# Order at the head of attention, ScalarE in emission order, and routing steps that carry over, in a fused attention and expert kernel

## The chip, the cores and the metric

One core of one Trainium2 chip. The metric is the device time of one execution in microseconds (us), median over the runs of one kernel. Every batch of experiments ran beside fresh runs of the kernel before, on the same chip.

## The reference, cut to what matters

Sliding-window attention (8 batches, 8 heads, 576 positions, head size 64, window 64) is followed by a layer of 8 experts. Each of the 4608 rows goes to exactly one expert, which depends on the row's logits and, by a second "local" gate, on the expert of the row before it.

```python
attn_out = _attn_ref(q, k, v)                      # softmax over 64 earlier positions
x = attn_out.transpose(0, 2, 1, 3).reshape(B, S, H * D)
logits = x @ w_gate;  local_gate = sigmoid(x @ w_local)
for b in range(B):
    prev_e = -1
    for s in range(S):
        fresh_e = argmax(logits[b, s])
        e = fresh_e if s == 0 or local_gate[b, s] < 0.5 else prev_e
        prev_e = e
        h = relu(x[b, s] @ w1[e])
        out[b, s] = softmax(logits[b, s])[e] * (h @ w2[e])
```

## The kernel before

Attention runs over 9 superchunks of 512 rows, each in 4 units (pairs of heads). A unit's scores are emitted two units ahead of its values. The gate logits come from `vt`, a second, turned copy of v that only the gates read. The values also read `vb`, v moved by 64 positions, which ScalarE copies. After half of the rows are done, the routing of the first half (which row goes to which expert, as a table `idx`) is worked off in 15 pieces, squeezed between the attention units. Then the rows of the first expert block are gathered by an indirect DMA with `idx`, and the experts run.

```python
HALF = 0.8
...
def turned(sc):                                   # vt of a superchunk, one buffer
    vtt = vts[sc] = kp.tile([P, HP, SC], F32, name="vtt", bufs=1)
    nc.sync.dma_start(out=vtt, in_=vt[:, :, sc * SC:(sc + 1) * SC])
turned(0); load(0); load(1)                       # load: k and q by pairs, then v3
...
gated = gates(0)                                  # TensorE, reads vt; copy on ScalarE
turned(1)
for move in spread(0, *gated): move()             # transposes, then the vb copies on ScalarE
units = [(sc, hp) for sc in range(NSC) for hp in range(HP)]
ps = {u: scores(*u) for u in units[:LEAD]}        # the first scores and exponentials

def step():                                       # called twice in each unit
    nonlocal pause
    if side and pause <= 0:
        pause = next(side, (0.0, False))[0]       # a routing piece, with its weight in us
    pause -= HALF

for i, (sc, hp) in enumerate(units):
    ...                                           # scores of unit i + 2, vb copies
    step(); values(sc, hp, ...)
    if hp == 0: gated = gates(sc + 1); turned(sc + 2)
    step()
    if hp == HP - 1:
        ...                                       # store of the superchunk's rows to xs, on GpSimd's queue
        if side is None and 4 * (sc + 1) >= C1: side = rt.first(psum)
for _ in side:                                    # what is left of the routing
    pass
ex.begin()                                        # gathers and weights of the first two expert blocks
```

The four tiles of the buffer ring hold k and q of the superchunks first and expert weights afterwards. So the second block's weights (two matrices of 2 MB) can only be loaded when the last scores are done, at about 142 us. At the end a flag is tested, and a slow fallback path follows in a branch that isn't taken.

## Time and profile before

| | |
|---|---|
| time, median of 3 runs | 752.04 us (751.59 to 752.31) |
| span in the profile | 750.2 us |
| TensorE busy | 691.8 us, 92% |
| routing table ready, gather issued | 147.97, 148.25 us |
| last attention matmul ends | 148.67 us |
| first expert matmul | 161.26 us |
| last matmul of the program | 742.42 us |

Read the table as two stages with a hole between them. TensorE is full in the expert stage, so only an earlier start of it can shorten the run. The start hangs on a chain: the table, the gather, the transposes of the gathered rows. The lines that show this are in the prediction.

### The profile page before, as it was taken

To read this page: it belongs to the slowest core of one execution; us is meant where nothing else is said; L and a number is where in the kernel's file an instruction comes from. 1 tells how busy PE (TensorE), PEld (TensorE's weight loads), DVE (VectorE), ACT (ScalarE), POOL (GpSimd) and SP (SyncE) were. 2 spreads that over 40 slices of the span, in tenths; PEclk is the share of its full clock that TensorE was granted. 3 is DMA by queue.
4 is the path that set the end of the run, shared out by engine and by line. 5 is a ranking of instruction groups with operands and counts; after the bars stand their busy time and mean duration, and the time that the engine had idled before them with its cause. 6 is when DMAs were issued, how large, how long until landed. Compare 5 with 4: busy or idle time off the path is not lost. (4 is left out here: it accounts for less than half of the span.)

```text
span 750.2 us, 12553 instructions
## 1 busy us (share of the span) xinstructions
PE 691.8 (92%) x5479; PEld 502.4 (67%) x5479; DVE 182.7 (24%) x426; ACT 145.8 (19%) x186; POOL 92.8 (12%) x109
## 2 busy tenths in 40 slices
PE   3788787749999999999999999999999999999995
PEld 2666666647677767567567567576776777677673
DVE  4576788923730011011010010010010001001000
ACT  2667665401111101101101101100110110010010
POOL 2000000111132111111110110111111111010010
PEclk9799999969999999999999999999999999999998
DMA  9999996867889964644654643689889898888601
GB/s 327 388 393 399 395 388 251 321 245 251 325 313 382 423 268 142 241 178 140 231 186 139 225 187 141 216 308 348 307 332 328 307 343 307 319 295 310 225 15 31
DMA packets 37331, 203.84 MB, mean 272 GB/s; under 512 B 3437, under 2 KB 3453, under 8 KB 29072
## 3 DMA queue, kind: packets, MB, share of 16 engines
q1 hardware_dynamic: 28320, 173.45, 63.1%
q0 software_dynamic: 8944, 29.45, 9.9%
q8 instruction: 47, 0.77, 0.4%
q14 instruction: 20, 0.16, 0.1%
HBM read 184.01 MB, written 19.92 MB: 272 GB/s over the span
## 5 line engine op out<-in xcount | busy, mean ns | idle before, releaser
L872 PEld LDWEIGHTS hp<-xt,w 128*128 128x128 f32 x2048 | 274.8, 193 | 28.3 <-issue 14.3
L872 PE MATMUL hp<-xt,w 128*128 128x128 f32 (+1 forms) x2048 | 289.9, 303 | 0.7 <-ACT xt L860 0.7
L886 PE MATMUL yp<-w,h 128*128 128x512 f32 x640 | 280.4, 592 | 0.0
L886 PEld LDWEIGHTS yp<-w,h 128*128 128x128 f32 x640 | 118.9, 190 | 136.8 <-issue 134.9
L876 DVE TENSOR_SCALAR h<-hp 128x512 f32<-128x512 f32 x34 | 23.5, 691 | 473.5 <-issue 362.0
L891 ACT ACTIVATE y<-yp,pw 128x512 f32<-128x512 f32 x40 | 27.5, 687 | 358.3 <-PE yp L886 342.2
L892 POOL DMA_INDIRECT out_dram<-y,idx x40 | 41.8, 1045 | 302.6 <-ACT y L891 275.8
L840 POOL DMA_INDIRECT xg<-xs,idx x40 | 39.1, 977 | 217.3 <-PE tp L859 188.4
L878 ACT ACTIVATE h<-hp 128x512 f32<-128x512 f32 x46 | 27.5, 597 | 163.0 <-PE hp L872 163.0
L238 PE MATMUL sp<-w 64*64 64x128 f32 (+1 forms) x1296 | 46.4, 278 | 13.7 <-issue 8.4
L238 PEld LDWEIGHTS sp<-w 64*64 64x64 f32 x1296 | 39.7, 142 | 22.8 <-issue 14.4
L267 PE MATMUL xo<-vb,p 128*64 128x74 f32 x576 | 46.8, 233 | 8.3 <-issue 4.3
L267 PEld LDWEIGHTS xo<-vb,p 128*64 128x64 f32 x576 | 40.8, 138 | 11.5 <-issue 4.8
L267 PE MATMUL xo<-va,p 128*64 128x74 f32 x576 | 47.0, 234 | 1.5 <-issue 1.5
L257 DVE TENSOR_TENSOR p<-p,mask 128x1024 f32<-128x1024 f32 x36 | 43.9, 1221 | 12.1 <-ACT p L254 11.9
L267 PEld LDWEIGHTS xo<-va,p 128*64 128x64 f32 x576 | 40.8, 138 | 2.7 <-issue 2.7
L254 ACT ACTIVATE p<-sp 128x1024 f32<-128x1024 f32 x36 | 36.7, 1022 | 15.7 <-PE sp L238 14.1
L859 PE MATMUL tp<-ident,xg 128*128 128x128 f32 x160 | 23.2, 277 | 10.8 <-DMA xg<-xs,idx 10.8
L859 PEld LDWEIGHTS tp<-ident,xg 128*128 128x128 f32 x160 | 18.9, 143 | 11.8 <-issue 11.0
L209 PE MATMUL xo<-vtt,wg2s 128*32 128x512 f32 x72 | 12.5, 705 | 13.9 <-DMA wg2s<-in_wg_dram 8.3
L276 DVE TENSOR_TENSOR x<-xo,allr 128x512 f32<-128x512 f32 x36 | 24.5, 680 | 0.0
L322 POOL DMA_DIRECT2D xs<-x x9 | 6.9, 764 | 130.3 <-DVE x L276 116.2
(198 smaller groups left out, 201.5 us busy)
## 6 DMA issues: line engine op xcount, KB each, us to landing
w<-in_w_dram SPq DMA_DIRECT2D x64, 2048.0 KB, 8.7
va<-in_v_dram SPq DMA_DIRECT2D x9, 1184.0 KB, 12.6
vtt<-in_vt_dram SPq DMA_DIRECT2D x9, 1024.0 KB, 11.1
xs<-x POOLq DMA_DIRECT2D x9, 1024.0 KB, 10.2
w<-in_k_dram SPq DMA_DIRECT2D x8, 1024.0 KB, 13.1
w<-in_q_dram SPq DMA_DIRECT2D x8, 1024.0 KB, 15.0
w<-in_k_dram SPq DMA_DIRECT2D x4, 256.0 KB, 6.1
w<-in_q_dram SPq DMA_DIRECT2D x4, 256.0 KB, 5.8
```

What stands on the lines that cost most here:

```text
L238: nc.tensor.matmul(sp[c * WIN:(c + 1) * WIN, j, a:b], lhsT=kt[h, hp, block * WIN:(block + 1) * WIN], rhs=qt[h, hp, a:b], start=True, stop= ...
L254: nc.scalar.activation(p, sp, Act.Exp, scale=DH ** -0.5)
L257: nc.vector.tensor_tensor(p, p, m.to_broadcast([P, 2, SC]), op=Alu.mult)
L267: nc.tensor.matmul(xo[par * WIN:(par + 1) * WIN, j, s * VW:(s + 1) * VW], lhsT=p[:, j, b * WIN:(b + 1) * WIN], rhs=w[:, s, 2 * hp + j, :], ...
L276: nc.vector.tensor_tensor(x[:, :, hp].rearrange("p c j d -> p j c d"), o[:, :, :, :DH], rr.to_broadcast([P, 2, 4, DH]), op=Alu.mult)
L840: nc.gpsimd.indirect_dma_start(out=x, out_offset=None, in_=self.xs[:rows, :], in_offset=bass.IndirectOffsetOnAxis(ap=idx[:, s:s + 1], axis=0))
L859: nc.tensor.transpose(tp[:, kk, :], x[:, kk * P:(kk + 1) * P], self.ident)
L872: nc.tensor.matmul(hp[:, i, :], lhsT=st["w1"][:, kk, m * P:(m + 1) * P], rhs=st["xt"][:, kk, :n], start=(kk == 0), stop=(kk == DK - 1))
L878: nc.scalar.activation(o, hp, Act.Relu)
L886: nc.tensor.matmul(yp, lhsT=st["h"][:, m, i * P:(i + 1) * P], rhs=st["w2"][:, m, :], start=(m == 0), stop=(m == FK - 1))
L891: nc.scalar.activation(y, yp, Act.Copy, scale=st["pw"][:, s:s + 1])
L892: nc.gpsimd.indirect_dma_start(out=self.out[:, :], out_offset=bass.IndirectOffsetOnAxis(ap=st["idx"][:, s:s + 1], axis=0), in_=y, in_offse ...
```

## The change

It has four parts. The routing steps carry their remaining allowance over to the next call (before, a `pause` below zero was overwritten and so lost), and the first fetch moves into the loop. The first two units' scores are emitted before the first gates, and the small gate weights are loaded earlier. ScalarE keeps the order in which the program emits its instructions. The loads of a superchunk are ordered by need.

```diff
+    wg2s = const.tile([P, HP, GW], F32, name="wg2s")     # moved up from behind zrow
+    nc.gpsimd.dma_start(out=wg2s, in_=wg2)
...
-    ctx.enter_context(tc.manual_schedule(engines={ET.PE}))
+    ctx.enter_context(tc.manual_schedule(engines={ET.PE, ET.Activation}))
...
-    turned(0)
-    load(0)
-    load(1)
+    load(0, [slice(0, 1), slice(1, 2), "turned", "values", slice(2, 3), slice(3, 4)])
+    load(1, ["values", pairs])
...
+    units = [(sc, hp) for sc in range(NSC) for hp in range(HP)]
+    ps = {u: scores(*u) for u in units[:LEAD]}
     gated = gates(0)
-    turned(1)
+    load(1, ["turned"])
     for move in spread(0, *gated):
         move()
-    units = [(sc, hp) for sc in range(NSC) for hp in range(HP)]
-    ps = {u: scores(*u) for u in units[:LEAD]}
...
     def step():
-        nonlocal pause
-        if side and pause <= 0:
-            pause = next(side, (0.0, False))[0]
+        nonlocal pause, side
         pause -= HALF
+        if side and pause <= 0.0:
+            w, trip = next(side, (0.0, None))
+            pause = max(pause, -HALF) + w
+            if trip is None:
+                side = ()
+                ex.begin()
...
-            if sc + 2 < NSC:
-                load(sc + 2)                              # at the head of the superchunk
...
             if sc + 2 < NSC:
-                turned(sc + 2)
+                load(sc + 2, ["turned", "values", pairs])
...
-    for _ in side:
-        pass
-    ex.begin()
+    while side:
+        step()
```

More of the change, by code (lines that the diff above doesn't have):

```diff
@@ L94 @@
     ok = const.tile([P, 1], F32, name="ok")
-    wg2s = const.tile([P, HP, GW], F32, name="wg2s")
-    nc.gpsimd.dma_start(out=wg2s, in_=wg2)
     moe = xs, w1, w2, out, tabs, lt, ident
@@ L154, in attention, with load @@
     ps_x = ctx.enter_context(tc.tile_pool(name="at_ps_x", bufs=2, space=PSUM))
-    ctx.enter_context(tc.manual_schedule(engines={ET.PE}))
+    ctx.enter_context(tc.manual_schedule(engines={ET.PE, ET.Activation}))
     qts, kts, vts, vas, vbs = {}, {}, {}, {}, {}
-    def load(sc):
+    def load(sc, parts):
         t = slice(sc * SC, (sc + 1) * SC)
-        both = ring.tile([P, 2, HP, SC], F32, name="w")
-        kt, qt = kts[sc], qts[sc] = both[:, 0], both[:, 1]
-        va = vas[sc] = kp.tile([P, 4, H, VW], F32, name="va")
-        step = 1 if sc == 0 else HP
-        for i in range(0, HP, step):
-            h = slice(i, i + step)
-            nc.sync.dma_start(out=kt[:, h], in_=k[:, h, t])
-            nc.sync.dma_start(out=qt[:, h], in_=q[:, h, t])
-        nc.sync.dma_start(out=va, in_=v3[t].rearrange("(c p) h x -> p c h x", p=P))
-    def turned(sc):
-        vtt = vts[sc] = kp.tile([P, HP, SC], F32, name="vtt", bufs=1)
-        nc.sync.dma_start(out=vtt, in_=vt[:, :, sc * SC:(sc + 1) * SC])
-    turned(0)
-    load(0)
-    load(1)
+        for part in parts:
+            if part == "turned":
+                vtt = vts[sc] = kp.tile([P, HP, SC], F32, name="vtt", bufs=1)
+                nc.sync.dma_start(out=vtt, in_=vt[:, :, t])
+            elif part == "values":
+                va = vas[sc] = kp.tile([P, 4, H, VW], F32, name="va")
+                nc.sync.dma_start(out=va, in_=v3[t].rearrange("(c p) h x -> p c h x", p=P))
+            else:
+                if sc not in kts:
+                    both = ring.tile([P, 2, HP, SC], F32, name="w")
+                    kts[sc], qts[sc] = both[:, 0], both[:, 1]
+                nc.sync.dma_start(out=kts[sc][:, part], in_=k[:, part, t])
+                nc.sync.dma_start(out=qts[sc][:, part], in_=q[:, part, t])
+    pairs = slice(0, HP)
+    load(0, [slice(0, 1), slice(1, 2), "turned", "values", slice(2, 3), slice(3, 4)])
+    load(1, ["values", pairs])
     row = cp.tile([P, 1], I32, name="row")
```

## The prediction

> **What bounds the kernel now.** I read the page's slices first, then busy time by engine in stretches, then the instructions in order of time around the place where attention hands over to the experts.
>
> ```profile
> PE   3788787749999999999999999999999999999995
> PEclk9799999969999999999999999999999999999998
> DMA  9999996867889964644654643689889898888601
> ```
>
> One digit is 18.8 us. From slice 9 (about 169 us) to the end TensorE never falls below 90%: this is the expert stage, and its length is TensorE's work. No part of the change touches it, so it can only start earlier. All that can be won lies in the first eight or nine slices. Stretches of that part (columns: length, PE, PE weight load, DVE, ACT, POOL busy, clock, DMA share, GB/s):
>
> ```profile
> 20.00:100.00 80.00, 64.61 (x1536) 52.09 (x1536) 55.04 (x107) 52.38 (x57) 3.80 (x5) 0.94 1.04 394
> 100.00:120.00 20.00, 15.53 (x367) 12.48 (x367) 16.78 (x47) 13.09 (x14) 0.75 (x1) 1.00 1.01 378
> 126.00:140.00 14.00, 10.02 (x244) 8.07 (x247) 13.54 (x35) 7.77 (x8) 0.75 (x1) 1.00 0.98 370
> 150.00:160.00 10.00, 0.50 (x3) 0.53 (x4) 2.50 (x10) 0.00 (x0) 1.41 (x2) 0.61 1.01 414
> 160.00:165.00 5.00, 4.32 (x20) 3.92 (x19) 0.90 (x5) 0.91 (x2) 0.97 (x1) 0.50 0.28 93
> ```
>
> Until 100 us the DMA engines are full (1.04, 394 GB/s) and ScalarE is busy only 52.4 of 80 us; from 126 to 140 us VectorE is the full one (13.54 of 14); from 150 to 160 us nothing computes. That hole is the largest single loss:
>
> ```profile
> 141.78 0.75 POOL L322 DMA_DIRECT2D xs<-x  x1 [13.60 <-DVE x L276]
> 148.25 1.04 POOL L840 DMA_INDIRECT xg<-xs,idx  x1 [5.72 <-DVE idx L730]
> 159.50 1.08 PE L859 MATMUL tp<-ident,xg 128*128 128x128 f32 x4 [10.83 <-DMA xg<-xs,idx]
> 161.26 6.06 PE L872 MATMUL hp<-xt,w 128*128 128x128 f32 x32 [0.68 <-ACT xt L860]
> 167.37 3.74 PE L872 MATMUL hp<-xt,w 128*128 128x128 f32 x32
> ```
>
> The last attention matmul ends at 148.67. TensorE then waits 10.83 us for the gathered rows of the first expert block. The gather was issued at 148.25, when the routing table (idx) was ready, and landed 11.1 us later. The first block's weights were in time: issued at 125.2 and 128.7, landed after 9.5 and 12.5 us, so by 141.2. The first 32 expert matmuls take 6.06 us, the next equal 32 take 3.74.
>
> At the head:
>
> ```profile
> 8.26 1.94 PE L209 MATMUL xo<-vtt,wg2s 128*32 128x512 f32 x8 [8.26 <-DMA wg2s<-in_wg_dram]
> 12.01 3.70 PE L238 MATMUL sp<-w 64*64 64x128 f32 x72
> 20.00 1.94 ACT L254 ACTIVATE p<-sp 128x1024 f32<-128x1024 f32 x2
> 26.38 1.93 PE L209 MATMUL xo<-vtt,wg2s 128*32 128x512 f32 x8 [1.14 <-DMA vtt<-in_vt_dram]
> ```
>
> Gates, scores and the vb copies stand in a row before the first exponential at 20.0. At 26.38 TensorE waits for the second superchunk's vt.
>
> **What the Trainium skill says.** "TensorE: Matmul & The Clock Gate", Part 1, gives half the clock after an idle window of about 3.4 us and the full clock again after as long a busy one. The trace agrees: 0.50 in 160 to 165 us, and 6.06 against 3.74 us. "DMA: Bandwidth & Descriptors", Issuing engines are not separate DMA queues, says that all issuers share the same 16 DMA engines. The trace agrees: the gather shared them with 4 MB of weights issued at 142 and a 1 MB store. The same page, Two DMAs through the same engine are not ordered, says that descriptors of one queue start in order; here the store issued at 141.78 landed after 16.4 us (158.2), and the gather behind it on the same queue at 159.3. "Runtime: NRT & Kernel Launch", Instruction fetch mechanics, says instructions are refilled in 16 KiB blocks and this is mostly hidden. The page shows 47 such packets; TensorE has unexplained gaps of 0.8 to 1.8 us about every 6.4 us while the DMA engines are full, which would fit refills that are not hidden. No run shows that cause, and the change doesn't touch it.
>
> **The change part by part.** Instruction counts, matmuls and bytes stay the same; I take no time off for work removed.
>
> 1. Routing steps that carry over. Each step of the routing has a weight in us, each call pays 0.8. Before, a remainder below zero was thrown away. Counted from the code with the 15 weights (sum 17.8): the last piece comes out at call 30 of 32 before, at call 23 after. Two calls make a unit, calls start in unit 20. So idx moves from just after unit 34 to just before unit 31's normalisation; the built program's VectorE order says the same. Fetching the first blocks also moves inside the loop, and on GpSimd's queue the two gathers now stand ahead of the store of superchunk 7, not behind it. The stretch from idx to the last attention matmul: before, unit 31's normalisation at 140.81 to 148.67, or 7.9 us, of which 0.9 was the table's end; estimate 7 to 7.5. A gather that isn't behind a store landed in 3.1 us (issued at 160.9) to 7.9 us (beside weights). It should land just before or at the end of attention. Then TensorE runs on: transposes 0.7, copy 0.6, hand-overs 0.15, so the first expert matmul starts 1.45 us after 148.67, at 150.1 in place of 161.26: 11.1 us. With no gap of over 3 us the clock stays up: 6.06 - 3.74 = 2.3 us. Sum 13.4 us.
>
> 2. Scores before gates, vt no longer first, wg2s first. The head's chain gets shorter: scores can start at about 6 us, exponentials are no longer behind the vb copies, and I estimate the first values at 17 in place of 23.0. But the gates of superchunk 1 stand next in TensorE's order and need vt of superchunk 1. Ahead of it in the queue are the same 7.7 MB as before (two superchunks of k, q, v3 and one vt). At 0.39 MB per us it lands at 26.4 before and within 0.5 us of that after. So 6 us are won and waited away. I count 0.3.
>
> 3. ScalarE in emission order. Before, three vb copies (1.18 each) often ran ahead of an exponential. Until 97 us TensorE never waited for it: its gaps there are of the unexplained kind. After 97 us VectorE waited for exponentials 0.74 + 0.32 + 0.34 + 0.43 = 1.8 us; I take half, 0.9.
>
> 4. Loads in the order of need. From superchunk 5 the built queue again reads k, q, v3, vt, as before; earlier vt moves ahead of q. With a full queue and 48 MB in all no byte comes sooner on the whole. 0.
>
> 5. VectorE from unit 20 to 35. Its work (about 50 us out of 55) is unchanged, only squeezed to the front; it stays the bound from 100 to 148 us. Denser PSUM round trips of the routing may cost as much as calmer last units give. 0, give or take 2.
>
> Sum: 13.4 + 0.3 + 0.9 = 14.6. I hold back 0.3 for a gather that sometimes lands late: 14.3. Predicted time 752.04 - 14.3 = 737.7 us, 1.9% less.
>
> **The rivals.** (a) The head's 6 us survive to the end of attention: 732. For it: DVE and ACT get earlier work. Against: DMA at 1.04 until 112 us, and the wait for vt at 26.38. (b) The gather lands late still, as its packets meet the second block's weights, issued after the last scores (142.1 before): 3 to 6 us of the hole stay, 741 to 744. Against: those weights need about 10 us, and the gather is ahead of them. (c) The squeezed routing makes TensorE and VectorE wait for each other through the two shared PSUM buffers: attention ends 2 to 3 us later, 740. For it: five round trips in calls 3 to 8 in place of 5 to 11. (d) Emission order blocks exponentials behind a copy that waits; a us or two.
>
> **Range and chances.** The 13.4 us are a measured hole and sure to 1.5 us; the attention stretch is open by 2 to 3 us either way. 80%: 733.5 to 741.5. The border of 2% is at about 737.1, just below my number: faster 0.45, within 2% 0.54, slower 0.01.
>
> **What would show it.** Right: no wait of TensorE for xg over 1.5 us; the first 32 expert matmuls in about 3.7 us; idx about 7 us before the last attention matmul; the expert stage about 579 us from its first matmul, the start of which is near 149; the first values at 17 but the second gates still at about 26, waiting for vt. Wrong: second gates well before 25 us (a); an xg wait of several us (b); the last attention matmul after 150 (c, d), or before 146.

## The result

The changed kernel takes 739.10 us (median of 4 runs, 737.77 to 740.69); the runs of the kernel before beside it have a median of 751.82. The ratio is 0.9834, with a 95% interval of 0.9811 to 0.9858. A ratio is the mean time of one kernel's fast runs over the mean of the other's in the same rounds, so it isn't quite the ratio of the medians quoted. The result is correct, and by the border of 2% the verdict is "within 2%".

The slices of the page after (40 slices of 18.4 us, digits in tenths):

```profile
PE   5588878899999999999999999999999999999995
PEclk9999999999999999999999999999999999999999
DMA  9999999699899965455355446588998898888500
```

The dip to 4 at slice 8 of before is gone: TensorE is at 90% or more from slice 8 on. The place of the hand-over, from the timelines of GpSimd and TensorE (start, duration, engine, line and operation, idle time before it and what ended it):

```profile
141.84 1.04 POOL L841 DMA_INDIRECT xg<-xs,idx  x1 [11.61 <-DVE allr L272]
145.22 0.82 POOL L324 DMA_DIRECT2D xs<-x  x1
...
146.66 0.65 PE L860 MATMUL tp<-ident,xg 128*128 128x128 f32 x4
150.13 3.81 PE L873 MATMUL hp<-xt,w 128*128 128x128 f32 x32 [1.21 <-ACT xt L861]
154.00 3.74 PE L873 MATMUL hp<-xt,w 128*128 128x128 f32 x32
```

The second block's weights in SyncE's queue, first before, then after:

```profile
142.12 1.02 SPq L846 DMA_DIRECT2D w<-in_w_dram  x2
```

```profile
143.57 1.02 SPq L847 DMA_DIRECT2D w<-in_w_dram  x2
```

The gather goes out 6.4 us earlier (141.84 against 148.25), and now 1.7 us ahead of these weights, not 6.1 us behind them. It lands after 3.6 us in place of 11.1. Its rows are there when TensorE reaches the transposes (no wait on that line), and the transposes even fit in ahead of the last attention matmuls, which end at 148.93. What is left of the hole is 1.21 us for the copy. The sum of the two traces:

| | before | after | difference |
|---|---|---|---|
| end of attention's matmuls | 148.67 | 148.93 | +0.26 |
| from there to the first expert matmul | 12.59 | 1.20 | -11.39 |
| first expert matmul to the last matmul (742.42, 729.04) | 581.16 | 578.91 | -2.25 |
| sum | | | -13.38 |

The spans differ by 750.2 - 736.8 = 13.4 us, so nothing is missing. The 2.25 us are the clock: the first 32 expert matmuls take 3.81 in place of 6.06 us (granted clock 1.00 from 150 to 154 us after, 0.50 from 160 to 165 us before).

The head went otherwise. The kernel after, TensorE and the queue of SyncE (the six lines stand at three places of its timelines):

```profile
4.36 1.99 PE L238 MATMUL sp<-w 64*64 64x128 f32 x36 [4.36 <-DMA w<-in_q_dram]
16.54 0.39 PE L267 MATMUL xo<-vb,p 128*64 128x74 f32 x1
28.66 1.94 PE L209 MATMUL xo<-vtt,wg2s 128*32 128x512 f32 x8 [8.99 <-DMA vtt<-in_vt_dram]
43.09 1.07 PE L209 MATMUL xo<-vtt,wg2s 128*32 128x512 f32 x8 [0.91 <-PE xo L267]
...
13.21 2.02 SPq L164 DMA_DIRECT2D vtt<-in_vt_dram  x1
30.65 0.54 SPq L164 DMA_DIRECT2D vtt<-in_vt_dram  x1
```

The first values start at 16.54 in place of 23.0. Then the gates of the second superchunk wait 8.99 us for `vt` and start at 28.66, 2.3 us later than before; the third gates start at 43.09 in place of 39.64. The load of the second `vt` was issued at 13.21; before, it was:

```profile
11.67 2.52 SPq L173 DMA_DIRECT2D vtt<-in_vt_dram  x1
```

Its only buffer becomes free when the first gates have read it. These now stand behind the first scores, wait 0.91 us for their own `vt`, and end at 12.11, in place of 10.20. From issue to landing the load took 15.3 us (before: 14.7). The clock column of this trace is not to be trusted in the head: it says 1.00, but 8 gate matmuls took 1.94 us at 28.66 and 1.07 at 43.09, and 36 score matmuls 1.99 us at 30.53 and 1.12 at 37.34. So TensorE ran at half pace after the wait.

The stretches show what lies between. Columns: length, busy time of PE, weight loads, DVE, ACT and POOL, clock, DMA share, GB/s. First before, then after:

```profile
30.00:32.00 2.00, 2.00 (x53) 1.75 (x56) 1.40 (x2) 1.96 (x2) 0.00 (x0) 1.00 1.05 390
32.00:34.00 2.00, 2.00 (x70) 1.85 (x65) 1.28 (x5) 1.98 (x3) 0.00 (x0) 1.00 1.05 393
40.00:42.00 2.00, 1.73 (x37) 0.85 (x30) 1.97 (x5) 0.59 (x1) 0.62 (x1) 1.00 1.02 379
```

```profile
30.00:32.00 2.00, 2.00 (x34) 1.47 (x34) 0.00 (x0) 0.58 (x1) 0.00 (x0) 1.00 0.87 315
32.00:34.00 2.00, 2.00 (x26) 1.55 (x20) 0.35 (x1) 1.36 (x2) 0.00 (x0) 1.00 0.97 276
40.00:42.00 2.00, 2.00 (x68) 1.93 (x68) 1.25 (x3) 1.67 (x2) 0.00 (x0) 1.00 0.75 208
```

Before, the DMA engines were full in all three stretches. After, they fall to 276 and 208 GB/s. The load of the third `vt` (issued at 30.65, before at 28.37) has to wait until the second gates have read the only buffer, and whatever stands behind it in SyncE's queue waits with it. In the new order that includes 1 MB of q (issued at 31.23), which the old order had issued ahead of that `vt` (16.84). Experiment e3 tells the two apart. The gates of the next four superchunks start 1.8 to 3 us later than before. By the end of attention only 0.26 us of this is left.

### The profile page after: what moved, and what is told of

Its sections match the earlier page's. It is cut to its first block, busy times and chain, and to the rows that moved or that the text cites. A ratio compares the mean times of both kernels' runs of the same rounds, so it can differ in the third digit from the quotient of the medians.

```text
span 736.8 us, 12546 instructions
## 1 busy us (share of the span) xinstructions
PE 690.8 (94%) x5479; PEld 501.8 (68%) x5479; DVE 181.3 (25%) x426; ACT 146.4 (20%) x186; POOL 93.9 (13%) x109
## 5 line engine op out<-in xcount | busy, mean ns | idle before, releaser
L267 PE MATMUL xo<-vb,p 128*64 128x74 f32 x576 | 49.0, 238 | 7.9 <-issue 3.8
L267 PE MATMUL xo<-va,p 128*64 128x74 f32 x576 | 49.3, 238 | 3.3 <-issue 3.3
L267 PEld LDWEIGHTS xo<-vb,p 128*64 128x64 f32 x576 | 42.2, 142 | 14.6 <-issue 10.2
L267 PEld LDWEIGHTS xo<-va,p 128*64 128x64 f32 x576 | 42.3, 142 | 1.8 <-issue 1.7
L209 PE MATMUL xo<-vtt,wg2s 128*32 128x512 f32 x72 | 12.2, 704 | 13.4 <-DMA vtt<-in_vt_dram 9.9
L861 DVE COPY xt<-tp 128x512 f32<-128x512 f32 x32 | 21.2, 680 | 0.0
## 6 DMA issues: line engine op xcount, KB each, us to landing
vtt<-in_vt_dram SPq DMA_DIRECT2D x9, 1024.0 KB, 11.4
```

The lines of the kernel that those rows point to most:

```text
L267: nc.tensor.matmul(xo[par * WIN:(par + 1) * WIN, j, s * VW:(s + 1) * VW], lhsT=p[:, j, b * WIN:(b + 1) * WIN], rhs=w[:, s, 2 * hp + j, :], ...
```

## The experiments

The theory after the result: the whole gain is the carry-over; it puts the gather ahead of the second block's weights and so takes it out of the hand-over. The other three parts are worth nothing together. (The expectations of e1 to e3 went further and held that the head costs 2 us; that did not come true.) The rivals: the head's gain hides a loss elsewhere, ScalarE's order has a worth of its own, or the gather was late for another reason than the weights, namely the store ahead of it in its queue, which the prediction had named.

### e1: the kernel before with the carry-over alone

```diff
# before.py, only step() and the end of the loop, as in the change
+        pause -= HALF
+        if side and pause <= 0.0:
+            w, trip = next(side, (0.0, None))
+            pause = max(pause, -HALF) + w
+            if trip is None:
+                side = ()
+                ex.begin()
```

> The kernel before with the routing steps that carry over (and the fetch of the first blocks inside the loop) as its only change. Theory A (the hole at the handover is the whole gain, the head's parts gain nothing and cost 2 us): idx about 7 us before the last attention matmul, no wait for the gathered rows, second gates at 26.4 us as before, time 736.5 to 738.5, so 1 to 2.5 us below the changed kernel. Rival B (ScalarE's order and the head also carry some of the gain): 740 to 745.

Measured: 739.47 us (738.57 to 740.75), ratio 0.9832 (0.9813 to 0.9851), beside a before of 752.24. The table was ready at 139.15, the last attention matmul ended at 149.06, the first expert matmul started at 150.39. So this part alone gives the whole change. I had expected one to three us less, as the head was held to cost 2 us. It costs nothing that shows: here the second gates start early, at 26.34 as in the kernel before, and attention still ends as in the changed kernel (149.06 against 148.93); e12 says the same. One place in the trace may have cost this run time: TensorE idled 1.79 us at 135.7 to 137.5, waiting for VectorE, which was copying the routing's result, and the clock fell after it. The same columns as above:

```profile
136.00:137.00 1.00, 0.00 (x0) 0.00 (x0) 1.00 (x3) 0.97 (x2) 0.00 (x0) 1.00 0.15 49
137.00:138.00 1.00, 0.49 (x12) 0.52 (x14) 0.97 (x7) 0.12 (x1) 0.00 (x0) 0.89 0.08 33
138.00:139.00 1.00, 1.00 (x22) 1.00 (x20) 1.00 (x2) 0.00 (x0) 0.00 (x0) 0.50 0.07 16
```

VectorE is full in these lines, TensorE does nothing in the first, and the clock has fallen to 0.50 in the last; it stays there until 141 us. What this cost was not tested.

### e2: the changed kernel without the carry-over

```diff
# after.py, with step() and the end of the loop of before
+        if side and pause <= 0:
+            pause = next(side, (0.0, False))[0]
         pause -= HALF
...
+    for _ in side:
+        pass
+    ex.begin()
```

> The changed kernel with the old routing steps: scores first, loads and ScalarE's order are kept. Theory A: the hole is back (gather issued near the end of attention, 8 to 11 us wait of TensorE, cold clock after it), and the head costs 2 us: 752 to 755. Rival B: 745 to 750.

Measured: 752.38 us (751.77 to 753.22), ratio 1.0003 (0.9987 to 1.002). The wait for `xg` was back with 8.19 us, and the first 32 expert matmuls took 6.08 us. Head, ScalarE order and loads together are worth nothing without the carry-over. Attention ended at 150.92 in this profile, 2.25 us later than before, and the gathered rows landed later still, at 158.9. With e1 this settles where the gain comes from.

### e3: the changed kernel with the loads in the old order

```diff
-    load(0, [slice(0, 1), slice(1, 2), "turned", "values", slice(2, 3), slice(3, 4)])
-    load(1, ["values", pairs])
+    turned(0)
+    load(0)
+    load(1)
...
+            if sc + 2 < NSC:
+                load(sc + 2)
...
-                load(sc + 2, ["turned", "values", pairs])
+                turned(sc + 2)
```

> The changed kernel with only the loads put back (vt of superchunk 0 first, the old queue order); scores still first, ScalarE in emission order, steps carry over. Theory A (the new load order starves the DMA queue near 30 and 40 us and lets vt of superchunk 1 land at 28.5 in place of 26.4 us): second gates back to about 26.4 us, attention ends up to 2 us sooner, time 736.5 to 738.5. Rival C (the later end of the head is made good by slack that follows, as VectorE is the bound later): within 0.7 us of the changed kernel.

Measured: 739.60 us (738.62 to 742.16), ratio 0.984 (0.9815 to 0.9865). The second gates started at 27.86 after a wait of 6.88 us for `vt`. The same columns as above:

```profile
32.00:34.00 2.00, 2.00 (x42) 1.60 (x44) 1.17 (x2) 1.95 (x3) 0.00 (x0) 0.85 1.04 392
40.00:42.00 2.00, 1.13 (x32) 0.98 (x32) 1.97 (x4) 1.03 (x1) 0.00 (x0) 1.00 1.08 394
```

With the old order the DMA engines are full, although the single buffer and the late second gates are still there. So the dips to 276 and 208 GB/s need the new order; a late reader alone does not make them (e8, with the old order and its second gates at 27.60, is full there too, and e2, with the new order, falls to 279 GB/s from 40 to 42 us). But filling them gains no time: rival C holds. The order doesn't bring `vt` of superchunk 1 sooner either: it is issued at 13.11, behind the first gates, and lands at about 28 us.

### e4 and e11: a second buffer for vt, loaded early

The remedy for the wait at the head: two buffers, and `vt` of superchunk 1 directly behind the first superchunk's pieces. Room for it was made by moving two mask constants into a temporary pool and by letting a late scratch tile share another's space (not shown).

```diff
# after.py
-                vtt = vts[sc] = kp.tile([P, HP, SC], F32, name="vtt", bufs=1)
+                vtt = vts[sc] = kp.tile([P, HP, SC], F32, name="vtt", bufs=2)
...
-    load(1, ["values", pairs])
+    load(1, ["turned", "values", pairs])
...
-    load(1, ["turned"])
```

> The changed kernel with two buffers for vt (room made by giving two index tiles back early), so vt of superchunk 1 is loaded right behind that of superchunk 0's pieces, before v3, k and q of superchunk 1. Theory A (TensorE's 9 us wait at 19.7 us is a wait for this one transfer): second gates at 19 to 21 us in place of 28.7, the wait then moves in part to k and q of superchunk 1, and full DMA engines limit what is left: attention ends 2 to 4 us sooner, 735 to 737. Rival C (stages after the head have the slack to hide it): no change, 738.5 to 739.5.

> The kernel of e4 (two vt buffers, vt of superchunk 1 loaded right behind the first pieces) once more, in five rounds, to settle whether it beats the changed kernel. Theory A: 735.5 to 737.5, ratio to the kernel before below 0.981, the second gates near 19 and the first expert matmul near 148.8. Rival: e4 fell well by chance, and this is within 1 us of the changed kernel's 739.1.

Measured: e4 736.66 us (734.24 to 737.12), ratio 0.978 (0.9759 to 0.9802); e11, the same kernel in five rounds, 734.93 us (734.19 to 738.03), ratio 0.9783 (0.9762 to 0.9805), with a before of 751.83. Both results are correct. It beats both kernels, and the changed one by about 0.5% by the ratios (0.978 against 0.9834). The gates of e4, on TensorE:

```profile
19.19 1.07 PE L212 MATMUL xo<-vtt,wg2s 128*32 128x512 f32 x8
37.71 1.06 PE L212 MATMUL xo<-vtt,wg2s 128*32 128x512 f32 x8
```

The wait of 8.99 us is gone and the second gates start 9.5 us earlier. By the third gates 5.4 us of that remain, and of the whole time 2.4 us in e4 and 4.2 in e11. The DMA engines are full again in this stretch (399 GB/s from 30 to 32 us, 406 from 40 to 42); as e3 is full there too and no faster, that by itself is not the gain. The second buffer and the earlier place in the queue were changed together, and neither was run alone. A second lesson lies in the pair: the same kernel's first expert matmul started at 148.77 in one profile and at 146.41 in the other (on another chip). Single landmarks of one trace scatter by a us or two, so I don't read smaller differences from them.

### e5: the last two stores on another queue

The prediction had read the gather's 11 us as a wait behind the store in GpSimd's queue. Here the stores go out from ScalarE.

```diff
# before.py
-            nc.gpsimd.dma_start(out=xs[...], in_=x[...])
+            (nc.scalar if sc >= NSC - 2 else nc.gpsimd).dma_start(out=xs[...], in_=x[...])
```

> The kernel before with the stores of the last two superchunks issued from ScalarE's queue and not from GpSimd's, so that the first gather no longer stands behind a 1 MB store on its queue. Routing steps as before, idx still at 148. Theory A (of the 11.1 us from the gather's issue to its landing a part is the store ahead of it on the same queue): landing 6 to 8 us, TensorE's wait 6 to 8 in place of 10.8 us, time 748 to 750. Rival D (all queues share the 16 engines, so the store and 4 MB of weights slow the gather wherever they are issued): 10 to 11 us, 751.5 to 752.5.

Measured: 760.28 us (758.47 to 762.14), ratio 1.0119. The gather was issued at 148.49, TensorE still waited 10.08 us for it, and the first expert matmul started at 160.18. So the store's queue isn't what holds the gather; for the wait, rival D holds. But the run is 8 us slower although its last matmul comes 1.8 us *earlier* than before. The last GpSimd line of each, first before, then e5, each below its span:

```profile
span 750.2 us, 12553 instructions
...
743.17 0.98 POOL L892 DMA_INDIRECT out_dram<-y,idx  x1 [11.82 <-DVE bad L132]
```

```profile
span 758.5 us, 12550 instructions
...
q10 hardware_dynamic: 1056, 2.10, 0.7%
...
741.33 0.98 POOL L893 DMA_INDIRECT out_dram<-y,idx  x1 [13.03 <-DVE bad L132]
```

From the end of the last instruction to the end of the span it is 6.05 us before (750.2 - 744.15) and 16.19 in e5 (758.5 - 742.31). The page lists a DMA queue more, q10, with the 2.1 MB of the two stores. That the 10 us belong to that queue fits, as nothing else of the program's end changed; what is done in them the profile doesn't show.

### e6: the carry-over, but a table only five calls later

```diff
# after.py; the last piece comes out at call 28 of 32 instead of 23
-HALF = 0.8
+HALF = 0.65
```

> The changed kernel with 0.65 in place of 0.8 as what one call pays off, so that the routing ends at call 28 and not 23: idx about 5 us later, at about 145 to 146, and the gather again behind the store of superchunk 7. Theory A: the gather lands 8 to 11 us after its issue, so near 154 to 156; TensorE's wait is 5 to 7 us, with a cold clock after it: 745 to 748. Rival E (the gather has slack, as it landed 3.6 us after its issue and 3.5 us ahead of the last attention matmul): 740 to 742.

Measured: 753.61 us (753.33 to 753.80), ratio 1.0031. I missed by 6 us. The table was ready at 149.10, attention ended at 150.15, the second block's weights had been issued at 143.2, and:

```profile
144.10 0.75 POOL L324 DMA_DIRECT2D xs<-x  x1 [12.41 <-DVE x L276]
149.38 1.04 POOL L841 DMA_INDIRECT xg<-xs,idx  x1 [4.53 <-DVE allr L272]
...
160.59 1.09 PE L860 MATMUL tp<-ident,xg 128*128 128x128 f32 x4 [10.44 <-DMA xg<-xs,idx]
162.35 6.04 PE L873 MATMUL hp<-xt,w 128*128 128x128 f32 x32 [0.67 <-ACT xt L861]
```

The carry-over is worth nothing if the gather goes out after the weights. The gain isn't spread over the calls; it is a step between call 23 and call 28.

### e7: ScalarE's order alone

```diff
# before.py, in attention
-    ctx.enter_context(tc.manual_schedule(engines={ET.PE}))
+    ctx.enter_context(tc.manual_schedule(engines={ET.PE, ET.Activation}))
```

> The kernel before with ScalarE in emission order as the only change. As I predicted: 0.9 us less, from VectorE's waits for exponentials after 97 us; all of it is an earlier end of attention. Theory F (TensorE's gaps and full DMA engines set the pace to 97 us, VectorE's work after it, so ScalarE's order is hidden): within 0.7 us of before, with other waits of VectorE for exponentials in place of those.

Measured: 749.48 us (748.33 to 749.85), ratio 0.9976 (0.9951 to 1.0002), so not told apart from no change with confidence. The table was ready 1.4 us earlier (146.54), the last attention matmul ended 0.45 us earlier, and the first expert matmul started at 158.49. What it may give comes mostly by way of the gather. In this profile the granted clock was 0.50 from 145 us to the end of attention, so it is a weak witness for the end of attention.

### e8: scores before gates alone

```diff
# before.py; vt still first in the queue
+    units = [(sc, hp) for sc in range(NSC) for hp in range(HP)]
+    ps = {u: scores(*u) for u in units[:LEAD]}
     gated = gates(0)
```

> The kernel before with the first two units' scores emitted ahead of the first gates, as the only change (vt still first in the queue). Theory A (second gates wait for vt of superchunk 1 whatever stands before): first values up to 2 us earlier than 23.0, second gates at 26.3 to 28, time within 1 us of before. Rival B (the head's gain survives): 2 to 5 us less.

Measured: 755.13 us (751.06 to 756.38), ratio 1.004 (0.9997 to 1.0083). The first values started at 17.72, the second gates at 27.60 after a wait of 6.11 us. The early start wins nothing, and a small loss is possible but not certain.

### e9: the second block's weights cut to an eighth

This measures the disputed wait by itself. The result of one expert block is wrong on purpose (the relative error was 0.41); the number and the shapes of the matmuls stay.

```diff
# before.py
-            nc.sync.dma_start(out=t, in_=w[bass.ds(e, 1)].rearrange("o p x -> (o p) x"))
+            part = slice(0, D if n == -2 else a * b)
+            nc.sync.dma_start(out=t[:, part], in_=w[bass.ds(e, 1)].rearrange("o p x -> (o p) x")[:, part])
# and the block's matmuls read those columns again and again
```

> The kernel before, with only 256 KB of each of the two weight matrices of the second expert block loaded (0.5 MB in place of 4 MB; the result of that block is wrong on purpose, the number and shapes of its matmuls are the same). Theory A: the gather of the kernel before lands about 11 us after its issue because it shares the DMA engines with 4 MB of weights and a 1 MB store issued 5 to 6 us ahead of it; 5 MB at the 0.4 MB per us that the stretch shows are 12.5 us, 1.5 MB are under 4. So with the weights cut the gather should be issued near 148.3 as before, land in 3 to 5 us, the first expert matmul start at 152.5 to 154.5 instead of 161.3, its first 32 take below 4.5 us and the whole be 741 to 745. Rival B: the store ahead of it in GpSimd's queue, or the gather of scattered rows itself, sets the 11 us; then the gather lands after 8 us or more and the whole stays above 748.

Measured: 743.92 us (743.02 to 744.13), ratio 0.9886 (0.987 to 0.9903). The view of the tile `xg`, narrowed to 138 to 165 us, gives the time from the gathers' issue to landing; before, then e9:

```profile
DMA to landing us min/median/max: 3.1/10.5/11.1
```

```profile
DMA to landing us min/median/max: 3.3/3.3/3.3
```

TensorE's lines of e9:

```profile
151.62 1.09 PE L860 MATMUL tp<-ident,xg 128*128 128x128 f32 x4 [3.04 <-DMA xg<-xs,idx]
153.38 6.07 PE L873 MATMUL hp<-xt,w 128*128 128x128 f32 x32 [0.68 <-ACT xt L861]
```

The gather was issued at 148.16, as before, behind the same store in the same queue, and landed after 3.3 us in place of 11.1. So it was the weights in flight that made it slow; that they did so by holding up the store ahead of it is ruled out by e5, where no store stood in its queue and the wait stayed. The first expert matmul comes 7.9 us earlier, and the time is 7.9 us less (751.83 to 743.92). The last 2.3 us, those of the clock, are not won, against my expectation of less than 4.5 us for the first 32 matmuls: the clock was 0.50 from 151.5 us on, after a wait of 3.04 us.

### e10: the routing squeezed further

```diff
# after.py; the last piece comes out at call 19
-HALF = 0.8
+HALF = 1.0
```

> The changed kernel with each call paying 1.0 in place of 0.8, so that the routing ends at call 19 in place of 23 (28 with 0.65). Theory A: the hole in front of the experts is already closed at 23, so an earlier table is worth nothing; idx comes 6 to 8 us earlier (near 134), the attention end stays within 1 us of 148.9, the whole within 1.5 us of the changed kernel: 737.5 to 740.5. Rival C: squeezing the routing into fewer calls is what costs the carry-over 1 to 2 us of the hole's worth; then this costs again 1 to 3 us: the last attention matmul after 150 and the whole 740.5 to 743.

Measured: 738.57 us (737.08 to 739.48), ratio 0.9813 (0.9794 to 0.9831). The table was ready at 136.32, the last attention matmul ended at 149.44. Five more us of lead are worth nothing once the hole is closed, and squeezing the routing doesn't cost anything that could be told apart.

### e12: carry-over and ScalarE's order, with the old head

```diff
# e1, and in attention
+    ctx.enter_context(tc.manual_schedule(engines={ET.PE, ET.Activation}))
```

> The kernel before with the carry-over and ScalarE's emission order, and with its own head and order of loads: the changed kernel without its two head parts. Alone, the carry-over gave 739.5 and ScalarE's order 749.5, of which the gain came by an earlier table and gather more than by an earlier end of attention. Theory A: that gain is the hole's again, and once the hole is closed nothing or little of it is left; 738.3 to 740, the last attention matmul at 148.5 to 149.2. Rival: ScalarE's order has a worth of its own, which the head's loss hides in the changed kernel: 736.3 to 737.5, the last attention matmul before 147.5.

Measured: 738.35 us (737.83 to 738.86), ratio 0.9837 (0.9809 to 0.9865), against 0.9832 for the carry-over alone. The last attention matmul ended at 148.27. Once the hole is closed nothing of e7's possible gain is left, and the head of the changed kernel hides none.

## Why the prediction was right or wrong

The time was inside the range, 1.4 us above the number, and the argument about the bound held: TensorE's expert stage was only shifted.

1. **Carry-over, 13.4 us: right, in both terms.** The hole closed by 11.4 us less 0.26 of a later attention end (11.1 predicted), and the clock gave 2.25 (2.3 predicted). The table came 6.4 us earlier, 7.4 us ahead of the last attention matmul, about 7 foreseen; the first expert matmul came at 150.13, as the working says (150.1; the list of signs says 149). e1 gets 12.8 us by this part alone (752.24 to 739.47), e2 none without it.
   **One premise of this step was wrong.** The prediction put the store on the gather's queue beside the weights as the reason for the 11 us, and its estimate of the new landing rested on a gather "that isn't behind a store". In e5 the store was taken out of the queue and the wait stayed at 10.08 us; in e9 the store stayed and the weights went, and the gather landed after 3.3 us. The gain was right because the change puts the gather ahead of the weights as well, by 1.7 us; as far as the landing was reckoned from the store, the hit was luck. Rival (b), a late landing although the gather is ahead, did not come true (3.6 us). e6 shows how narrow the margin is: there, five calls later, the gather is behind the weights and a wait of 10.44 us stays.
   **A second premise is not safe:** that the clock stays up with no gap of over 3 us. It stayed up here, with a gap of 1.21 us, but in e1 it fell to 0.50 after one of 1.79 us.
2. **Head, 0.3 us: not told apart from zero, and one step was wrong.** The first values came at 16.54 as said (17). The second gates came at 28.66, not within 0.5 us of 26.4. The step that failed is "lands at 26.4 before and within 0.5 us of that after": it counted the bytes ahead of `vt`, and left out that the load can be issued only when the first gates have read the single buffer. The change puts those gates behind the scores and their own `vt` further back, so it was issued at 13.21 in place of 11.67 and landed about 2 us later. With a second buffer and an earlier place the wait is gone (e4). What the head is worth in the end is nothing that the runs can tell from zero (e2, e8, e12).
3. **ScalarE's order, 0.9 us: not confirmed.** Alone it gave about 2 us at the edge of the scatter, by an earlier gather (e7); beside the carry-over nothing (e12). It was counted as a term of its own, while its worth went through the same hole as term 1.
4. **Loads, 0: right in the time** (e3: 739.60 against 739.10), although the premise of a full queue did not hold: from 40 to 42 us the changed kernel moved 208 GB/s, with the old order 394.
5. **VectorE's stretch, 0 give or take 2: right in size.** Attention ended 0.26 us later, less than landmarks scatter. Rival (c), a squeeze that costs 2 to 3 us, falls with e10.

The terms 2 and 3 were to bring the end of attention 1.2 us forward, and it came 0.26 us later. That is 1.46 us of the 14.6 summed. The hand-over was 0.25 us shorter than worked out (1.20 against 1.45), because the transposes fitted in ahead of attention's last matmuls. This leaves the 13.4 us of the traces. The expert stage took 578.9 us, as predicted (579). Open stays why the late gates at the head leave so little trace at the end of attention: from 100 us on VectorE is the fullest of the compute engines (in the changed kernel 17.31 of 20 us from 100 to 120, 14.93 of 15 from 120 to 135), but no run separated it from the others.

## What to carry to other kernels

A small transfer on the critical path must be issued before the large ones that don't hurry: the same gather took 3.3 or 11 us, by what was in flight, and a few steps' delay in the program turned the whole gain of 13 us on or off. Gains that pass through one and the same wait don't add up; ask of each what is left of it when the wait is gone. And the bytes ahead of a load don't tell when it lands if its buffer has a reader: the load can't be issued before the reader is done. A second buffer, together with an earlier place in the queue, gained 2.4 and 4.2 us here (e4: 736.66, e11: 734.93 us), while the other order of the loads gained nothing (e3).

## What the Trainium skill lacked or had wrong

- "DMA: Bandwidth & Descriptors", Issuing engines are not separate DMA queues, says that issuing from several engines only saves time on the sequencer. It lacks a cost: two stores moved to ScalarE's queue lengthened the program's end from 6.05 to 16.19 us after its last instruction (e5). One kernel shows it; the cause is open. It has the sharing of the 16 engines right, but gives no number for what a small indirect transfer pays behind large ones: 128 rows took 3.3 us with 0.5 MB of weights issued shortly before, and 11.1 us with 4 MB (e9 and before).
- "TensorE: Matmul & The Clock Gate", Part 1, gives an idle window of about 3.4 us before the clock halves. Here an idle time of 3.04 us (e9) and one of 1.79 us (e1) were followed by a clock of 0.50, while 1.21 us (the changed kernel) were not. The pace of the matmuls says the same: the first 32 expert matmuls took 6.07 us in e9 and 3.81 in the changed kernel, and 36 score matmuls of e1 took 1.12 us before the gap (at 134.06) and 1.92 after it (at 139.48). The page's window is not a gap below which one is safe.
